# Sums of squares and scale exponents kept in spare PSUM columns, and only the last small VectorE step writing SBUF

## The chip, the cores and the metric

The kernel runs on one core of a Trainium2 chip. The metric is the device time of one execution in microseconds (us), lower is better. The engines are TensorE (PE in the profile, PEld for its weight loads), VectorE (DVE), ScalarE (ACT), GpSimd (POOL) and SyncE (SP, which issues most DMAs).

## The reference

Two stages, in float32. The first is a long convolution with gates: `u = x * v`; a filter `h_filt = (relu(pos_emb @ w1) @ w2) * exp(-0.01 * pos)`; `y = irfft(rfft(u) * rfft(h_filt))`, causal, over 12480 positions, for 2 batches and 128 channels; output `x * y`. The second is a feed-forward block on the 24960 tokens that come out: `h = x @ w_in` (128 to 2048), `g = max(h, 0) + alpha * min(h, 0)`, `g @ w_out`.

## The kernel before

Phase A computes the convolution by matmuls, as a Fourier transform of length 24960 = 195 x 128 in stages, with data split into two float16 parts (a high part and the remainder). The 128 channels come in two groups of 64. For each group **stage 1** forms `u`, scales it, splits it and multiplies with the table `t1`; **stage 2** (lines 674 to 808) multiplies with twiddles and with the filter's spectrum; **stage 3** (lines 813 to 874) goes back to tokens and stores to `g_d` in DRAM. Stage 1 of the second group runs together with stage 3 of the first. Phase B (from line 1024) finishes the transform per block of 390 tokens and runs the feed-forward block; it begins at about 640 us.

float16 has a narrow range, so each channel of `u` and of the filter gets a power-of-two scale. Stage 1 works in pairs of chunks (`u_pair`, 16 pairs per group, 32 in all; a pair is 8 channels): DMA loads x and v; `product` multiplies (L550, on DVE or POOL); `square` squares on ACT (L553); `norm` sums squares over the partitions on PE with a matrix of ones into a bank `mb` of PSUM (L561, 8 matmuls); `gather` sums 128 columns of that bank to 8 on DVE (L565, into the SBUF tile `n2`); `scale` runs the three small instructions of `scales` on DVE (L325 shifts the exponent out of `n2` into the SBUF tile `sc_e`, L326 clips and negates it in place, L327 adds a bias and writes `s_u`, in SBUF); `scaled` multiplies u with the scale (L576, on DVE or POOL); then `high` on ACT (L582), `low` on DVE or POOL (L585), the 48 matmuls of `transform` on PE (L619 to L621), and the reading of their bank by ACT (L631) and DVE (L634). The filter calls `scales` once, for 128 channels: L325 to L327 on 128 columns, then L401 scales `w2b`, for which PE waits in L419.

Each engine runs its instructions in the written order. That order comes from a list planner (`Plan`) which gives each operation a cost, its inputs (`r`), its outputs (`w`) and rooms: the pool "m" has two rooms, the two banks `mb`. A room is free again 200 ns after the planned end of the last operation that names it; before the change that is `gather` for a pair, since `scale` does not name the bank. In the second group's plan rooms are given in a fixed order.

In stage 3 (together with the second group's stage 1) DVE reads PSUM in L851 and PE works in L834 to L836.

Of the kernel before, what the change touches and what calls it, by code (L numbers as in the profile page):

```python
# [8 lines left out]
F32 = mybir.dt.float32  # L9
# [3 lines left out]
I32 = mybir.dt.int32  # L13
AF = mybir.ActivationFunctionType
ALU = mybir.AluOpType
AX = mybir.AxisListType
# [5 lines left out]
D = 128  # L22
# [14 lines left out]
CC = 4  # L37
# [212 lines left out]
def act_ns(n, psum=False):  # L250
    return n / 1.2 + (51 if psum else 93)


def dve_ns(n, rate=1):
    return n / 0.96 / rate + 67
# [6 lines left out]
def dma_ns(n):  # L262
    return n / 360
# [23 lines left out]
def body(ctx, tc, A, out, stop=None, dbg=None):  # L287
    nc = tc.nc
    sy, ac, ve, po, te = nc.sync, nc.scalar, nc.vector, nc.gpsimd, nc.tensor
# [12 lines left out]
    s_h = const.tile([128, D], F32, name="s_h")  # L302
# [14 lines left out]
    def units(u, n=1, p=128):  # L317
        assert u >= FIRST or u + n <= FIRST
        t, u = (ring, u - FIRST) if u >= FIRST else (first, u)
        return t[:p, u:u + n].rearrange("p u e -> p (u e)")  # L320

    def scales(pool, n2, s_out, n):

        e = pool.tile([128, n], I32, tag="sc_e", bufs=2, name="sc_e")
        ve.tensor_single_scalar(out=e, in_=n2.bitcast(I32), scalar=24, op=ALU.logical_shift_right)  # L325
        ve.tensor_scalar(out=e, in0=e, scalar1=10, scalar2=-(1 << 23), op0=ALU.max, op1=ALU.mult)  # L326
        ve.tensor_single_scalar(out=s_out.bitcast(I32), in_=e, scalar=196 << 23, op=ALU.add)  # L327

    def filter_(P, pool, z, mm, mb):
# [21 lines left out]
        w = ib * NT  # L351
# [41 lines left out]
        nh = P.buf("m")  # L393
# [3 lines left out]
            ve.tensor_scalar(out=nb, in0=ones, scalar1=n1, scalar2=float(FO), op0=ALU.mult, op1=ALU.mult)  # L397

        def scaled():
            scales(pool, mb[nh.i][:, :D], s_h, D)  # L400
            ve.tensor_tensor(out=w2b, in0=w2b, in1=s_h.unsqueeze(1).to_broadcast([128, 2, D]), op=ALU.mult)  # L401

        P.op("DVE", 400, gather, r=[("nq", q) for q in range(nq)], w=["nb"])
# [2 lines left out]
        for g in range(1, len(w2s)):  # L406
            P.op("ACT", act_ns(2 * D), lambda g=g: ac.activation(w2s[g], w2b, AF.Copy, scale=float(np.exp(-DECAY * WJ * g))),
                 r=[("w2s", 0)], w=[("w2s", g)])
# [95 lines left out]

    def phase_a():
        ps = ctx_a.enter_context(tc.tile_pool(name="psa", bufs=1, space=PSUM))
        wk = ctx_a.enter_context(tc.tile_pool(name="wk", bufs=2))
        mm = [ps.tile([128, 1024], F32, name=f"mm{j}") for j in range(3)]
        mb = [ps.tile([128, 512], F32, name=f"mb{j}") for j in range(2)]
        zp = ctx_a.enter_context(tc.tile_pool(name="zp", bufs=1))  # L510
# [11 lines left out]
        def stage1(P, g, shared, U):  # L522
            def u_pair(n):

                nps = P.buf("m")
                more = not shared and n >= NCH // 2 and n // 2 % 2
                kind = ("x2", "v2", "sq1", "uhl2") if more else ("x", "v", "sq1", "uhl")
                x, v, sq = [P.buf(kind[0]) for _ in range(2)], [P.buf(kind[1]) for _ in range(2)], P.buf(kind[2])
                b, c = divmod(n * CC, CG)
                c += g * CG  # L530
                s = s_u[:, b, c:c + 2 * CC]

                def xr(j):
                    return units(U[x[j].pool][x[j].i], p=NT)

                def vr(j):
                    return units(U[v[j].pool][v[j].i], p=NT)

                def sqr():
                    return units(U[sq.pool][sq.i], p=NT).bitcast(BF16).rearrange("p (c i) -> p c i", i=NI)  # L540

                n2 = []

                for j in range(2):
                    def load(j=j):
                        sy.dma_start(out=xr(j), in_=A["xv"][g, n + j, :, 0, :])
                        sy.dma_start(out=vr(j), in_=A["xv"][g, n + j, :, 1, :])

                    def product(e, j=j):
                        either[e].tensor_tensor(out=xr(j), in0=xr(j), in1=vr(j), op=ALU.mult)  # L550

                    def square(j=j):
                        ac.activation(sqr()[:, j * CC:j * CC + CC].rearrange("p c i -> p (c i)"), xr(j), AF.Square)  # L553

                    P.op("DMA", dma_ns(2 * NT * 2048), load, r=stored if more else [], w=[x[j], v[j]])
                    P.op({"DVE": dve_ns(512), "POOL": 1225}, 0, product, r=[v[j]], w=[x[j]])
                    P.op("ACT", act_ns(512), square, r=[x[j], sq], w=[("sq", n, j)])

                def norm():
                    for m in range(8):  # L560
                        te.matmul(mb[nps.i][:, :128], ones[:NT], sqr()[:, :, 16 * m:16 * m + 16], start=m == 0, stop=m == 7)  # L561

                def gather():
                    n2.append(wk.tile([128, 2 * CC], F32, tag="n2", name="n2"))
                    ve.tensor_reduce(out=n2[0], in_=mb[nps.i][:, :128].rearrange("p (c e) -> p c e", e=16), op=ALU.add, axis=AX.X)  # L565

                def scale():
                    scales(wk, n2[0], s, 2 * CC)

                P.op("PE", 450, norm, r=[sq, ("sq", n, 0), ("sq", n, 1)], w=[nps], rows=98)  # L570
                P.op("DVE", 220, gather, r=[nps], w=[("s", g, n)])
                P.op("DVE", 450, scale, w=[("s", g, n)])
                for j in range(2):
                    def scaled(e, j=j):
                        u = xr(j).rearrange("p (c i) -> p c i", c=CC)
                        either[e].tensor_tensor(out=u, in0=u, op=ALU.mult,  # L576
                                                in1=s[:NT, j * CC:(j + 1) * CC].unsqueeze(2).to_broadcast([NT, CC, NI]))

                    h = P.buf(kind[3])

                    def high(j=j, h=h):
                        ac.activation(halves(h)[:, 0], xr(j), AF.Copy)  # L582

                    def low(e, j=j, h=h):
                        either[e].tensor_tensor(out=halves(h)[:, 1], in0=xr(j), in1=halves(h)[:, 0], op=ALU.subtract)  # L585

                    P.op({"DVE": 600, "POOL": 1001}, 0, scaled, r=[("s", g, n)], w=[x[j]])
                    P.op("ACT", act_ns(512), high, r=[x[j]], w=[h])
                    P.op({"DVE": 600, "POOL": 1113}, 0, low, r=[x[j]], w=[h])
                    transform(n + j, [h], split(h))  # L590

            def halves(h):
                return units(U[h.pool][h.i], p=NT).bitcast(F16).rearrange("p (h e) -> p h e", h=2)

            def split(h):
                return lambda c, part: halves(h)[:, part, c * NI:(c + 1) * NI]
# [12 lines left out]
            def transform(n, keys, data):  # L609
                pb = P.buf("mm")  # L610
                col = n * CC
                zb, cs = z[:, col // ZC], slice(col % ZC, col % ZC + CC)
                late = [("rt", q) for q in range(16)] if not shared and CG <= col < NU else []

                def product():
                    p = mm[pb.i].rearrange("p (c j) -> p c j", c=CC)
                    for c in range(CC):
                        o = p[:, c, :2 * NF]
                        te.matmul(o, data(c, 0), t1[:, 0], start=True, stop=False)  # L619
                        te.matmul(o, data(c, 0), t1[:, 1], start=False, stop=False)  # L620
                        te.matmul(o, data(c, 1), t1[:, 0], start=False, stop=True)  # L621

                def pv():
                    return mm[pb.i].rearrange("p (c j) -> p c j", c=CC)[:, :, :2 * NF].rearrange("p c (a f) -> p a f c", a=2)

                P.op("PE", 12 * 84, product, r=keys, w=[pb] + late, rows=98)

                cuts = (0, 2 * FB, NF) if n == NCH - 1 or shared and n == NC // CC - 1 else (0, NF)
                for x, y in zip(cuts, cuts[1:]):
                    def high(x=x, y=y):  # L630
                        ac.activation(zb[:, 0, :, x:y, cs], pv()[:, :, x:y], AF.Copy)  # L631

                    def low(x=x, y=y):
                        ve.tensor_tensor(out=zb[:, 1, :, x:y, cs], in0=pv()[:, :, x:y], in1=zb[:, 0, :, x:y, cs], op=ALU.subtract)  # L634

                    P.op("ACT", act_ns(8 * (y - x), True), high, r=[pb], w=[("z", n, x)])
                    P.op("DVE", dve_ns(8 * (y - x)), low, r=[pb], w=[("z", n, x)])
# [258 lines left out]
        with tc.tile_pool(name="pre", bufs=2) as pre:  # L896
            P = Plan(mm=3, m=2, pt=5, x=8, v=3, sq1=2, uhl=4, x2=4, v2=2, uhl2=2)
# [16 lines left out]
        for g in range(1, NG):  # L914
            P = Plan(mm=3, m=2, x=7, v=3, sq1=2, uhl=3, sn=2, gst=2)
# [20 lines left out]
        P = Plan(mm=3, sn=3, gst=3)  # L936
# [295 lines left out]
```

## Time and profile before

| | us |
|---|---|
| median of 3 runs | 1831.11 (1825.75 to 1833.94) |
| profiled execution | 1827.88 |
| its span, first to last instruction | 1826.0 |
| PE busy | 1726.7 (95%) |
| VectorE busy | 1435.6 (79%) |
| ScalarE busy | 1298.5 (71%) |
| GpSimd busy | 1112.2 (61%) |

The shares are means over stages that differ: phase B (from 640 us) is 1186 us of PE at work, while in phase A VectorE is the engine with the least idle time over long stretches. Durations of an instruction include time in which it is held after it began, so that instructions of one form with the same data size can have different lengths.

### The profile page before, as it was taken

What the parts mean: (1) busy time and instruction counts of PE and PEld (TensorE: products, weight loads), DVE (VectorE), ACT (ScalarE), POOL (GpSimd) and SP (SyncE); (2) the same over time, 40 slices, a digit from 0 to 9 for tenths busy, and PEclk for the clock granted to TensorE, in tenths of its full rate; (3) what the DMA queues carried; (4) which work ended last, traced back from release to release, by engine and by line L of the source; (5) the groups of instructions that cost most, each with busy time, mean ns of one, the idle gap of its engine ahead of it and who ended that gap; (6) DMA issues with size and microseconds to landing.
All of it is one profiled execution on the core that took longest, in us unless ns stands there. A gap on an engine that the chain in (4) does not pass through costs nothing.

```text
span 1826.0 us, 34019 instructions
## 1 busy us (share of the span) xinstructions
PE 1726.7 (95%) x13398; PEld 1652.1 (90%) x13398; DVE 1435.6 (79%) x1660; ACT 1298.5 (71%) x1976; POOL 1112.2 (61%) x736
## 2 busy tenths in 40 slices
PE   7998888798888899999999999999999999999998
PEld 5997777787777799999999999999999999999998
DVE  5569999998997767777777777777777777777775
ACT  6457676676664477777777777777777777777776
POOL 4456988776893165556555655666555655565564
PEclk8779999899998999999999999999999999999999
DMA  6343345774434941010210120102101112012000
GB/s 192 99 124 109 137 149 157 212 237 150 162 127 120 256 131 54 18 54 28 62 53 19 54 64 26 54 18 72 54 19 53 32 58 54 19 54 64 26 9 19
DMA packets 98582, 155.05 MB, mean 85 GB/s; under 512 B 7088, under 2 KB 65746, under 8 KB 96468
## 3 DMA queue, kind: packets, MB, share of 16 engines
q1 hardware_dynamic: 97060, 152.05, 27.2%
q8 instruction: 105, 1.72, 0.4%
q10 hardware_dynamic: 1360, 0.81, 0.1%
q14 instruction: 57, 0.47, 0.1%
HBM read 106.97 MB, written 45.88 MB: 84 GB/s over the span
## 4 chain that ended last, share of the span: by engine, by line
PE 62%; DVE 19%; ACT 7%; DMA 6%; issue 6%; POOL 1%; ACTq 0%; POOLq 0%; SPq 0%; DVEq 0%
PE hp L1063 25%; PE o L1063 23%; DVE ring L733 5%; PE mm L419 4%; DVE ring L1127 3%; DVE ring L743 3%; ACT ring L1126 3%; DMA g_d<-ring 2%; DVE z L634 2%; DVE g_lo L1134 1%; ACT g_hi L1133 1%; PE yp L277 1%; PE yp L278 1%; PE yp L279 1%; PE mm L834 1%
## 5 line engine op out<-in xcount | busy, mean ns | idle before, releaser
L1134 POOL TENSOR_TENSOR g_lo<-ring,g_hi 128x780 fp32r<-128x780 f32 x256 | 506.6, 1979 | 494.6 <-ACT g_hi L1133 494.6
L1127 DVE SCALAR_TENSOR_TENSOR ring<-ring,keep,hp 128x780 f32<-128x780 f32 x512 | 523.8, 1023 | 284.6 <-ACT ring L1126 278.5
L1126 ACT ACTIVATE ring<-hp 128x780 f32<-128x780 f32 x512 | 420.4, 821 | 290.6 <-PE hp L1063 290.6
L1063 PE MATMUL hp<-ah,w 128*128 128x390 f32 x2048 | 543.1, 346 | 7.7 <-DVE ring L1127 2.9
L1063 PE MATMUL o<-g_hi,w 128*128 128x390 f32 x2048 | 534.6, 342 | 0.3 <-ACT ot L1148 0.3
L1133 ACT ACTIVATE g_hi<-ring 128x780 fp32r<-128x780 f32 x512 | 434.9, 849 | 0.4 <-DVE ring L1127 0.4
L1063 PEld LDWEIGHTS hp<-ah,w 128*128 128x128 f32 x2048 | 371.3, 190 | 24.0 <-DVE ring L1127 21.3
L1134 DVE TENSOR_TENSOR g_lo<-ring,g_hi 128x780 fp32r<-128x780 f32 x256 | 380.2, 1485 | 0.0
L1063 PEld LDWEIGHTS o<-g_hi,w 128*128 128x128 f32 x2048 | 375.1, 189 | 0.6 <-ACT ot L1148 0.6
L1063 PE MATMUL o<-g_lo,w 128*128 128x390 f32 x1024 | 266.4, 341 | 0.5 <-POOL g_lo L1134 0.5
L1063 PE MATMUL hp<-alo,w 128*128 128x390 f32 x1024 | 266.7, 342 | 0.0
L1063 PEld LDWEIGHTS o<-g_lo,w 128*128 128x128 f32 x1024 | 188.5, 189 | 0.8 <-POOL g_lo L1134 0.8
L1063 PEld LDWEIGHTS hp<-alo,w 128*128 128x128 f32 x1024 | 188.8, 189 | 0.1
L1049 POOL TENSOR_TENSOR gl<-gt,gh 98x1024 f16<-98x1024 f32 x62 | 134.2, 2164 | 3.8 <-ACT gh L1048 3.8
L733 DVE TENSOR_TENSOR ring<-mm,ring 128x512 f32<-128x512 f32 (+2 forms) x204 | 125.9, 656 | 8.4 <-ACT ring L721 8.1
L760 POOL TENSOR_TENSOR z<-ring,z 128x512 f16<-128x512 f32 x96 | 119.0, 1240 | 4.1 <-ACT z L756 4.1
L834 PE MATMUL mm<-t,z 128*128 128x128 f16 x512 | 104.5, 235 | 16.5 <-DVE z L634 7.5
L738 POOL TENSOR_TENSOR ring<-ring 128x256 f32<-128x256 f32 (+1 forms) x98 | 91.7, 936 | 46.4 <-DVE ring L733 41.6
L756 ACT ACTIVATE z<-ring 128x512 f16<-128x512 f32 (+2 forms) x102 | 62.5, 613 | 72.3 <-DVE ring L743 49.1
L836 PE MATMUL mm<-t,z 128*128 128x128 f16 x512 | 103.9, 234 | 0.1
L835 PE MATMUL mm<-t,z 128*128 128x128 f16 x512 | 104.0, 234 | 0.0
L619 PE MATMUL mm<-t,ring 98*128 98x196 f16 x320 | 84.3, 264 | 17.1 <-DVE z L634 7.9
(142 smaller groups left out, 3206.4 us busy)
## 6 DMA issues: line engine op xcount, KB each, us to landing
g_d<-ring SPq DMA_DIRECT2D x32, 784.0 KB
gt<-g_d SPq DMA_DIRECT2D x16, 1568.0 KB
ring<-in_tw SPq DMA_DIRECT2D x37, 512.0 KB
ring<-in_xv SPq DMA_DIRECT2D x72, 196.0 KB
xt<-in_xt SPq DMA_DIRECT2D x31, 390.0 KB
out_t<-ot SPq DMA_DIRECT2D x31, 390.0 KB
first<-in_xv SPq DMA_DIRECT2D x56, 196.0 KB
first<-in_tw SPq DMA_DIRECT2D x13, 512.0 KB
```

The costliest lines, as they stand in the source:

```text
L733: ve.tensor_tensor(out=t[:, :, m], in0=p[:, :, m], in1=hs[:, a:a + 1, m].to_broadcast([128, 2, (b1 - b0) * 2 * ZC]), op=ALU.mult)
L738: e.tensor_tensor(out=ta[:, 0, m], in0=ta[:, 0, m], in1=tb[:, 1, m], op=ALU.subtract)
L760: e.tensor_tensor(out=zl, in0=v, in1=zh, op=ALU.subtract)
L834: te.matmul(o, hi, t3[:, 0], start=True, stop=False)
L835: te.matmul(o, hi, t3[:, 1], start=False, stop=False)
L836: te.matmul(o, lo, t3[:, 0], start=False, stop=True)
L1049: po.tensor_tensor(out=dl, in0=src, in1=dh, op=ALU.subtract)
L1063: te.matmul(o[:, b, :TOK], w, d[:, b], start=start and n == 0, stop=stop and n == 2)
L1126: ac.activation(neg, h, AF.Relu, scale=-1.0)
L1127: ve.scalar_tensor_tensor(out=acts[n], in0=neg, scalar=keep[:, f:f + 1], in1=h, op0=ALU.mult, op1=ALU.add)
L1133: ac.activation(gh, a, AF.Copy)
L1134: (ve, po)[n % 2].tensor_tensor(out=gl, in0=a, in1=gh.bitcast(F32), op=ALU.subtract)
```

## The change

The tile `sc_e` (exponents) and the tile `n2` (sums) are no longer made in SBUF; the pool `wk` goes. `gather` writes its 8 sums into columns 256 to 263 of the pair's own bank `mb`, L325 writes the exponents into columns 264 to 271, L326 works there in place, and L327 reads them there and writes `s_u` or `s_h` in SBUF as before. For the filter the exponents go to columns 128 to 255 of its bank. The operation `scale` now names the bank, so that the planner keeps the room until `scale` has ended.

```diff
-    def scales(pool, n2, s_out, n):
-        e = pool.tile([128, n], I32, tag="sc_e", bufs=2, name="sc_e")
+    def scales(e, n2, s_out):
+        e = e.bitcast(I32)
         ve.tensor_single_scalar(out=e, in_=n2.bitcast(I32), scalar=24, op=ALU.logical_shift_right)
         ve.tensor_scalar(out=e, in0=e, scalar1=10, scalar2=-(1 << 23), op0=ALU.max, op1=ALU.mult)
         ve.tensor_single_scalar(out=s_out.bitcast(I32), in_=e, scalar=196 << 23, op=ALU.add)
...
-            scales(pool, mb[nh.i][:, :D], s_h, D)
+            scales(mb[nh.i][:, D:2 * D], mb[nh.i][:, :D], s_h)
...
-        wk = ctx_a.enter_context(tc.tile_pool(name="wk", bufs=2))
...
+                def spare(j):
+                    return mb[nps.i][:, 256 + 2 * CC * j:256 + 2 * CC * (j + 1)]
+
                 def gather():
-                    n2.append(wk.tile([128, 2 * CC], F32, tag="n2", name="n2"))
-                    ve.tensor_reduce(out=n2[0], in_=mb[nps.i][:, :128].rearrange("p (c e) -> p c e", e=16), op=ALU.add, axis=AX.X)
+                    ve.tensor_reduce(out=spare(0), in_=mb[nps.i][:, :128].rearrange("p (c e) -> p c e", e=16), op=ALU.add, axis=AX.X)
 
                 def scale():
-                    scales(wk, n2[0], s, 2 * CC)
+                    scales(spare(1), spare(0), s)
...
-                P.op("DVE", 450, scale, w=[("s", g, n)])
+                P.op("DVE", 450, scale, r=[nps], w=[("s", g, n)])
```

## Rows read from the trace of the kernel before

**Rows 1.** Windows by stage: start:end, length, each engine's busy us, clock, DMA, GB/s.
```profile
0.00:114.00 114.00, 102.56 (x612) 90.68 (x613) 62.41 (x98) 58.11 (x102) 47.33 (x44) 0.78 0.42 129
114.00:172.00 58.00, 47.43 (x515) 44.65 (x512) 56.13 (x81) 47.07 (x73) 46.23 (x39) 0.94 0.42 129
...
297.00:440.00 143.00, 120.71 (x1510) 115.01 (x1510) 125.41 (x199) 99.43 (x220) 99.43 (x85) 0.93 0.69 207
...
640.00:1826.00 1186.00, 1177.15 (x7604) 1151.20 (x7602) 898.12 (x824) 892.25 (x1143) 693.34 (x348) 1.00 0.15 45
```

**Rows 2.** Waits of PE from 114 to 172: us in total, times, longest.
```profile
PE mm L619 <- DVE z L634: 7.6, 9, 2.5
```

**Rows 3.** Waits of PE from 297 to 440.
```profile
PE mm L834 <- DVE z L634: 7.5, 5, 2.9
PE mm L619 <- DVE ring L851: 5.4, 4, 2.2
```

**Rows 4.** Instructions of the tile sc_e: durations ns min/median/max, first and last start.
```profile
L326 DVE TENSOR_SCALAR sc_e<-sc_e x33: 170/1029/1286, 20.0 to 422.4; 128x8 int32<-128x8 int32 x32, 128x128 int32<-128x128 int32 x1
L325 DVE TENSOR_SCALAR sc_e<-n x32: 154/214/1026, 19.8 to 422.2; 128x8 int32<-128x8 int32 x32
L327 DVE TENSOR_SCALAR s_u<-sc_e x32: 170/172/1111, 20.2 to 422.6; 128x8 int32<-128x8 int32 x32
```

**Rows 5.** Windows of the tile sc_e alone: VectorE busy us, then clock, DMA, GB/s.
```profile
0.00:114.00 114.00, 11.03 (x27) 0.78 0.42 129
114.00:172.00 58.00, 10.38 (x24) 0.94 0.42 129
297.00:440.00 143.00, 24.42 (x48) 0.93 0.69 207
```

**Rows 6.** Timeline, 29 to 33: start, us, engine, line, operation, shapes, [idle before].
```profile
29.07 3.71 POOL L550 TENSOR_TENSOR ring<-ring,first 98x512 f32<-98x512 f32 x3
...
30.07 0.29 DVE L325 TENSOR_SCALAR sc_e<-mb 128x128 int32<-128x128 int32 x1 [0.89 <-PE mb L404]
30.40 1.24 DVE L326 TENSOR_SCALAR sc_e<-sc_e 128x128 int32<-128x128 int32 x1
31.67 1.19 DVE L327 TENSOR_SCALAR s_h<-sc_e 128x128 int32<-128x128 int32 x1
```

**Rows 7.** Lines L634 and L565, which read PSUM and write SBUF.
```profile
L634 DVE TENSOR_TENSOR z<-mm,z x99: 223/964/980, 33.2 to 434.8; 128x784 f16<-128x784 f32 x93, 128x64 f16<-128x64 f32 x3, 128x720 f16<-128x720 f32 x3
L565 DVE TENSOR_REDUCE n<-mb x32: 273/278/284, 19.5 to 421.9; 128x8 f32<-128x128 f32 x32
```

**Rows 8.** Timeline of PE from 33.3.
```profile
33.38 2.88 PE L419 MATMUL mm<-w2b,z 128*98 128x128 f32 x12 [0.53 <-DVE w2b L401]
```

**Rows 9.** Chain of waits by line, windows 114:146, 311:346 and 373:424 in turn.
```profile
by line: DVE z L634 45.1%; DVE ring L550 10.0%; DVE sc_e L326 8.8%; POOL ring L576 6.4%; DVE sc_e L325 6.2%; issue 5.7%; ACT z L631 5.4%; DVE s_u L327 5.1%; DVE ring L576 4.3%; DVE n L565 1.9%; PE mm L619 1.6%; PE mm L621 1.1%; PE mm L620 1
by line: DMA g_d<-ring 31.7%; DVE ring L851 12.7%; DVE ring L576 8.8%; issue 8.0%; DVE z L634 7.9%; DVE sc_e L326 7.3%; DVE sc_e L325 5.9%; DVE ring L550 4.4%; DVE s_u L327 3.9%; PE mm L619 2.4%; ACT z L631 2.4%; PE mm L621 2.0%; PE mm L620
by line: DVE z L634 18.3%; DVE ring L851 12.7%; PE mm L834 8.2%; issue 8.2%; PE mm L835 7.2%; PE mm L836 7.1%; DVE sc_e L326 7.1%; PE mm L619 5.3%; PE mm L621 5.1%; PE mm L620 5.0%; DVE sc_e L325 2.8%; PE mb L561 2.7%; POOL ring L585 2.3%; 
```

**Rows 10.** Timeline, 154 to 163, of VectorE, GpSimd and PE.
```profile
154.81 0.52 DVE L325 TENSOR_SCALAR sc_e<-n 128x8 int32<-128x8 int32 x1
155.36 1.08 DVE L326 TENSOR_SCALAR sc_e<-sc_e 128x8 int32<-128x8 int32 x1
...
156.73 1.04 POOL L576 TENSOR_TENSOR ring<-ring,s_u 98x512 f32<-98x512 f32 x1 [0.31 <-DVE s_u L327]
...
161.74 1.01 PE L561 MATMUL mb<-ring,ones 98*128 98x128 bf16 x8 [2.54 <-ACT ring L553]
```

**Rows 11.** Lines L550 and L576 on VectorE, with two inputs from SBUF.
```profile
L550 DVE TENSOR_TENSOR ring<-ring,first x10: 672/693/1425, 27.4 to 404.9; 98x512 f32<-98x512 f32 x10
L576 DVE TENSOR_TENSOR ring<-ring,s_u x17: 675/875/1646, 21.9 to 424.4; 98x512 f32<-98x512 f32 x17
```

**Rows 12.** Timeline of VectorE and PE from 335.9.
```profile
335.91 1.35 PE L561 MATMUL mb<-ring,ones 98*128 98x128 bf16 x16
335.99 0.17 DVE L327 TENSOR_SCALAR s_u<-sc_e 128x8 int32<-128x8 int32 x1
```

More of the change, by code (lines that the diff above doesn't have):

```diff
@@ L540, in sqr @@
                     return units(U[sq.pool][sq.i], p=NT).bitcast(BF16).rearrange("p (c i) -> p c i", i=NI)
-                n2 = []
                 for j in range(2):
```

## The prediction

> **What bounds the kernel now.** I read the windows by stage first, since the page's mean shares mix stages. From 640 us PE is busy for 1177 of 1186 us, and nothing there is edited. The edited instructions stand in three stretches only: A, 0 to 114 us (the filter and the first pairs), B, 114 to 172 us (the rest of the first group's stage 1), C, 297 to 440 us (the second group's stage 1 beside stage 3). In B VectorE is busy for 56.1 of 58 us and PE for 47.4; in C VectorE for 125.4 of 143 and PE for 120.7 [rows 1]. The waits of PE say who leads: PE waits 7.6 us for L634 in B, and in C 7.5 us for L634 and 5.4 us for L851, both VectorE reading a bank that PE wants back [rows 2, 3]. So VectorE sets the pace of B and most of C. In A it doesn't: from 33.38 us on PE runs matmuls of L419 nearly without a gap, after an idle 0.53 us in which it waited for the filter's scales [rows 8].
>
> Then the tile view of the edited instructions. L326, on 8 columns, has a shortest duration of 170 ns and a median of 1029 [rows 4]. Such a difference at equal size is not work. The timeline shows its cause at 30 us: POOL runs three multiplications of L550 on end (29.07 to 32.78). In them, L325 reads 128 columns from PSUM, writes SBUF and takes 0.29 us; L326, on the same 128 columns from SBUF to SBUF, takes 1.24, and L327 1.19 [rows 6]. I read that as VectorE being held until a POOL instruction ends when it works SBUF to SBUF in this form, and not held when its input is PSUM. L565, PSUM to SBUF, agrees: 32 times between 273 and 284 ns, whatever POOL did [rows 7].
>
> **The change, part by part.** The number of instructions stays: 33 triples L325 to L327 and 32 L565.
>
> *Size of one small step.* L634 takes 964 ns for 784 columns and 223 for 64, so 741 / 720 = 1.03 ns a column [rows 7]. L325 from PSUM on 128 columns is 291 ns at most [rows 6], less 120 columns gives 167 ns for 8, beside 154 to 172 ns for an unheld step in SBUF [rows 4]. No row shows VectorE writing PSUM. From below 154 ns; from above 291 ns, the dearest unheld step here with a PSUM operand. I take 170, the nearest in size, so a step costs as before, without the hold. At the upper end 34 steps on the path (counted below) cost 34 x 0.12 = 4.1 us. L565 keeps its 278 ns.
>
> The Trainium skill, in "VectorE: DVE Perf Modes", section "The TRN2 errata", gives a PSUM source 62 cycles more of fixed cost than an SBUF source; as an estimate that is 65 ns a step, 2.2 us on the 34, and the time would be 1821.9. The 291 ns row speaks against it.
>
> *Whole gain on VectorE.* The steps are busy 11.03 + 10.38 + 24.42 = 45.8 us for 99 instructions [rows 5]; unheld 99 x 0.17 = 16.8, plus 0.3 for the filter's wide ones. 28.7 us of hold goes. How much of it counts goes by stretch.
>
> *A.* The filter's L326 and L327 fall from 2.43 to about 0.6 us, but PE idles only 0.53 us for them; the norms ahead of L419 fill the rest. Other triples there lie beside PE at work. Gain 0.5.
>
> *B.* The chain of waits from 114 to 146 gives L326, L325 and L327 8.8 + 6.2 + 5.1 = 20.1% of 32 us, 6.4 us [rows 9], in twelve pieces (four triples); unheld 12 x 0.17 = 2.0. Gain 4.4. After 146 the chain passes to POOL and PE, but POOL waits there for a scale: the triple at 154.81 is held 0.35 + 0.91 us, POOL's L576 starts right behind it, and through L550 and L553 PE's norm at 161.74, after 2.54 us of idle [rows 10]. Of 1.26 I count 0.9. B gives 5.3; all its hold would be 10.38 - 24 x 0.17 = 6.3.
>
> *C.* Chain from 311 to 346: 7.3 + 5.9 + 3.9 = 17.1% of 35 us = 5.98, twelve pieces, less 12 x 0.17 = 2.04, gain 3.9. From 373 to 424: 7.1 + 2.8 = 9.9% of 51 us = 5.05, ten pieces (L327's are unheld there), less 1.7, gain 3.3 [rows 9]. C gives 7.2; all its hold would be 24.42 - 48 x 0.17 = 16.3. Between 346 and 373 the chain runs over PE and I count nothing.
>
> *Holds that move.* Eight triples are followed at once by L550 or L576 on VectorE, which have two SBUF inputs and are held too: 672 and 675 ns unheld, up to 1425 and 1646 [rows 11]. Today the triple has often waited out the POOL instruction for them. Each may lose 0 to 0.97 us; I take the median excess of L576, 0.2, 1.6 in all.
>
> *The bank held longer.* `scale` now names the bank, so a norm must follow the scale of two pairs earlier. In the trace every norm already does, the closest being the second of the two that share the 16 matmuls at 335.91: it begins near 336.5, and the scale two pairs earlier ends at 336.16 [rows 12], itself a held one that ends earlier then. I cost it at nothing; if that cover fails it is the last rival. The freed pool and columns cost nothing: no DMA is added, and the instruction count of each engine is the same.
>
> Sum: 0.5 + 5.3 + 7.2 - 1.6 = 11.4 us. The profiled execution took 1827.9 (span 1826.0 and 1.9 around it), which gives 1816.5; it lies 3.2 below the median of the runs shown, so against that median 1819.7. What is late next is PE and ACT in C, and POOL's queue in B.
>
> **The rivals.**
>
> *The hold only moves to the last step.* L327 still writes SBUF. If a write to SBUF is what is held, L325 and L326 become short and L327 waits for the POOL instruction that L326 waits for today. The gain is then only the second and third holds of a triple, some 3 us on the path: 1828. For it: L327 has been held itself, up to 1111 ns [rows 4]. Against it: L325 from PSUM wrote SBUF unheld under POOL [rows 6]. This is also the case that the change doesn't do what it says.
>
> *Time freed on VectorE becomes idle time.* In C PE is busy 120.7 of 143 us, and ACT and the DMA of stores stand in the chain (31.7% of 311 to 346) [rows 1, 9]. If PE, ACT or POOL is just behind, half of C and a third of B go: 0.5 + 3.5 + 3.6 - 1.6 = 6.0, so 1825.
>
> *More than the chain shows.* PE's waits for VectorE in B and C are 20.5 us [rows 2, 3]; if all the hold of B and C turned into time, 0.5 + 6.3 + 16.3 - 1.6 = 21.5, 1810. For it: VectorE is the leader in both. Against it: the chain leaves VectorE for long pieces in C.
>
> *Slower: the planner writes another order.* A room of the pool m is free only when `scale` ends in the plan, some 0.5 to 2 us later than now. If the plan (which has its own costs, not those of the trace) finds the room shut, it puts a transform ahead of the norm, and that pair's scale, L576, L585 and matmuls all come later, with VectorE and POOL idle. The price is a PE wait as now seen behind L634, up to 2.9 us [rows 3], for each pair. From four pairs on the gain is gone; with eight in C 8 x 2.9 - 11.4 = +11.8, 1843. For it: one margin of 0.3 us [rows 12]. Against it: every other norm follows by 1.9 us or more.
>
> **How the numbers follow.** Chances: the forecast 0.45, hold moves 0.10, idle time 0.23, more than the chain 0.14, slower 0.08. 0.5% of 1831 is 9.2 us, about what a measurement can tell from no change, so faster means below 1822 and slower above 1840. The forecast, with its own 1814 to 1825 (upper step price, moved holds 0 to 0.97 each on half of the places), lies below 1822 in three quarters of its cases, 0.34; more than the chain adds 0.14 and idle time 0.08: faster 0.56. Slower has 0.07, its own case but for 0.01 where the loss only cancels the gain. The rest, 0.37, is the same. The range leaves out the far half of the large gain and the slower case: 1810 to 1831.
>
> **What would show it.** Right: no L326 above 0.25 us, L325 and L327 near 170 ns, 45.8 us of these steps near 17, B and C together about 12 us shorter, phase B as long as before. The hold moves: L327 with a median near 1 us. Idle time: steps short, but C no shorter and PE waiting for ACT or POOL. Another order: norms standing elsewhere among the matmuls, VectorE idle before L565. The forecast is wrong if the steps stay long, or if phase A ends within 5 us of where it ends now.

## The result, and the profile after

The changed kernel takes 1813.67 us (median of 4 runs, 1812.52 to 1817.52), the kernel before 1829.93 beside it. The ratio is 0.9915, 95% interval 0.9888 to 0.9942: 10.6 to 20.5 us less, 15.6 in the middle. The forecast was 11.4 us less. The profiled execution has a span of 1810.7 us, 15.3 below that of before. Every engine issues its instructions in the same order as before, so all differences come from how long they took and waited. (The edit moves line numbers: L550 is L547 after, L565 L564, L576 L575, L585 L584, L634 L633, L851 L850, L1063 L1062; L325 to L327 keep theirs.)

The small steps first: the view by tile `mb` of the kernel after, with durations in ns as min/median/max. It answers to [rows 4, 7].

```profile
L325 DVE TENSOR_SCALAR mb<-mb x33: 156/164/300, 21.1 to 409.9; 128x8 int32<-128x8 int32 x32, 128x128 int32<-128x128 int32 x1
L326 DVE TENSOR_SCALAR mb<-mb x33: 173/174/300, 21.3 to 410.1; 128x8 int32<-128x8 int32 x32, 128x128 int32<-128x128 int32 x1
L564 DVE TENSOR_REDUCE mb<-mb x32: 277/286/300, 20.8 to 409.5; 128x8 f32<-128x128 f32 x32
L327 DVE TENSOR_SCALAR s_u<-mb x32: 165/166/167, 21.5 to 410.3; 128x8 int32<-128x8 int32 x32
```

L326 had a median of 1029 ns, now 174; even its 128 columns take no more than 300 ns where they took 1.24 us [rows 6]. L327, which still writes SBUF, varies by 2 ns in 32 times. The steps' durations add up to 5.56 + 5.88 + 5.60 = 17.0 us, from 46.1 by the same sum. (The windows of [rows 5], which count overlaps once, have 45.8; they have 16.8 now.)

Next, where the time went. First matmul of each stage in the two traces (us), taken from the timeline of PE:

| | before | after | after minus before |
|---|---|---|---|
| last L419 of the filter | 109.5 | 110.2 | +0.7 |
| first group, stage 2 | 171.9 | 168.8 | -3.1 |
| stage 3 of it, beside stage 1 of the second | 301.0 | 297.9 | -3.1 |
| second group, stage 2 | 434.0 | 420.9 | -13.1 |
| last of stage 3 | 622.8 | 607.3 | -15.5 |
| first of phase B | 629.0 | 611.8 | -17.2 |
| end of the span | 1826.0 | 1810.7 | -15.3 |

B gave 3.8 us, C 10.0. The 2.4 us between 434 and 623 and the 1.7 behind it lie in unedited code, and phase B is 1.9 longer. In four kernels run below (the three variants of the small steps and the one with added shifts), which differ from this one only in the stretches A to C, the length from the second group's stage 2 to the last matmul of stage 3 was 187.3 to 189.5, beside 188.8 before and 186.4 here. I take that part as spread between executions; nothing shows it to be the change's.

Windows of B and C cut at these edges, the kernel before and then after (columns as in [rows 1]: PE, PEld, VectorE, ScalarE, GpSimd busy us).

```profile
113.60:171.90 58.30, 47.73 (x521) 44.95 (x519) 56.14 (x82) 47.32 (x73) 46.62 (x39) 0.94 0.43 130
297.10:435.00 137.90, 115.71 (x1450) 110.17 (x1450) 123.72 (x197) 96.53 (x215) 99.33 (x85) 0.93 0.68 204
```

```profile
114.50:168.80 54.30, 48.17 (x522) 45.20 (x520) 49.49 (x81) 46.74 (x73) 47.48 (x39) 0.93 0.46 144
294.00:421.90 127.90, 115.14 (x1451) 109.40 (x1450) 109.81 (x197) 96.28 (x216) 99.93 (x85) 0.93 0.73 219
```

VectorE's busy time fell by 6.7 us in B and 13.9 in C, that of PE, ScalarE and GpSimd hardly moved, and VectorE's idle time rose from 2.2 to 4.8 and from 14.2 to 18.1 us. So 4.0 of 6.7 and 10.0 of 13.9 us turned into time. PE's waits for VectorE in C were 14.2 us (7.5, 5.4, 0.7 and 0.6, from 301 to 435). Now they are 3.1, and a wait for a DMA, 0.7 us before, is longer than any of them (the kernel after, 297 to 435):

```profile
PE mm L618 <- DMA ring<-h_d: 3.9, 3, 1.8
PE mm L618 <- DVE ring L850: 1.5, 4, 0.6
PE mm L705 <- DVE z L633: 0.6, 1, 0.6
PE mm L618 <- DVE z L633: 0.6, 2, 0.4
PE mm L833 <- DVE ring L850: 0.4, 2, 0.2
```

(One more wait for VectorE, 2.8 us before and 2.5 after, stands ahead of the first small step of C and stays.)

C has 16 triples, the 17th to the 32nd of stage 1, so its parts can be compared between the same instructions (us, the number of a triple in brackets):

| part of C | before | after | gain | forecast |
|---|---|---|---|---|
| to the start of (17) | 10.0 | 9.5 | 0.6 | 0 |
| start of (17) to end of (22), 311 to 343 | 32.1 | 28.7 | 3.5 | 3.9 |
| end of (22) to start of (25), 343 to 373 | 29.5 | 25.5 | 4.0 | 0 |
| start of (25) to end of (32), 373 to 423 | 50.1 | 48.9 | 1.2 | 3.3 |
| from there to stage 2 | 11.2 | 10.4 | 0.8 | 0 |

The third and fourth parts went otherwise than forecast. Windows of these two, before and then after:

```profile
343.10:372.60 29.50, 24.74 (x297) 24.42 (x295) 24.20 (x37) 20.60 (x46) 19.96 (x17) 0.83 0.67 203
372.65:422.78 50.13, 42.86 (x575) 41.30 (x573) 47.97 (x80) 38.68 (x85) 42.76 (x37) 1.00 0.76 228
```

```profile
336.00:361.50 25.50, 25.09 (x326) 24.56 (x325) 22.42 (x37) 20.38 (x46) 20.24 (x17) 0.91 0.84 248
361.54:410.45 48.91, 44.23 (x567) 42.59 (x565) 40.83 (x80) 37.93 (x83) 43.06 (x37) 0.95 0.77 236
```

In the third part PE was idle for 4.8 of 29.5 us before and for 0.4 of 25.5 after. Its waits there were 2.9 us for L634 and 1.9 for L851, and the granted clock of the stretch was 0.83 before, 0.91 after: the idle time between held VectorE instructions had been followed by PE at 1.2 GHz. The chain of before showed this stretch as PE's, so I had counted nothing. In the fourth part VectorE is busy 7.1 us less, and 5.9 of that is idle time now. The chain of waits there (kernel after, 361.5 to 410, by line) says what took over:

```profile
by line: DMA first<-in_xv 32.7%; DMA ring<-h_d 17.3%; POOL ring L584 13.2%; issue 7.0%; PE mm L618 5.8%; POOL ring L547 5.6%; PE mm L620 5.0%; PE mm L619 4.8%; SPq L544 3.9%; SPq L543 3.3%; PE mb L558 3.0%; PE mm L834 1.6%; PE mm L833 1.6%;
```

No VectorE line stands in it. It is a loop: GpSimd's L584 reads the last of a buffer, SyncE can load the next x and v into it, GpSimd's L547 waits for them. A second thing happened at the end of this part: PE, which now waits for the loads of `h_d`, was idle for 1.84 us, and the granted clock, 1.00 in this part up to 405.3 us, was 0.50 (1.2 GHz) from there to its end, with PE on the chain. Timeline of PE:

```profile
402.35 0.61 PE L558 MATMUL mb<-ring,ones 98*128 98x128 bf16 x8
404.79 0.26 PE L618 MATMUL mm<-t,ring 98*128 98x196 f16 x1 [1.84 <-DMA ring<-h_d]
...
408.48 1.01 PE L558 MATMUL mb<-ring,ones 98*128 98x128 bf16 x8
```

Window from 405.3 to the end of the part:

```profile
405.30:410.45 5.15, 5.15 (x37) 4.47 (x35) 2.69 (x7) 3.20 (x5) 3.44 (x4) 0.50 0.42 122
```

In the kernel before, the whole part ran at 1.00. The eight matmuls of L558 took 0.61 us at the upper level and 1.01 at the lower; by that, as an estimate, some 2 of the 5.15 us can be the clock, about as much as this part fell short by. The runs do not separate it from the loop.

Holds that moved, in the list of groups of the whole span, before and then after (count | busy us, mean ns):

```profile
L576 DVE TENSOR_TENSOR ring<-ring,s_u 98x512 f32<-98x512 f32 x17 | 17.8, 1055 | 0.4
L550 DVE TENSOR_TENSOR ring<-ring,first 98x512 f32<-98x512 f32 x10 | 8.6, 856 | 0.0
```

```profile
L575 DVE TENSOR_TENSOR ring<-ring,s_u 98x512 f32<-98x512 f32 x17 | 19.2, 1137 | 0.4
L547 DVE TENSOR_TENSOR ring<-ring,first 98x512 f32<-98x512 f32 x10 | 10.8, 1083 | 1.6 <-DMA first<-in_xv 1.6
```

These two-input instructions got 3.6 us longer, 1.9 of it in the nine that stand right behind a triple (the prediction counted eight): some of the wait that a triple used to sit out falls on the next instruction with two SBUF inputs.

### The profile page after: what moved, and what is told of

Same layout as the page of the kernel before. It is cut to its first block, busy times and chain, and to the rows that moved or that the text cites. A ratio compares the mean times of both kernels' runs of the same rounds, so it can differ in the third digit from the quotient of the medians.

```text
span 1810.7 us, 34020 instructions
## 1 busy us (share of the span) xinstructions
PE 1727.5 (95%) x13398; PEld 1653.5 (91%) x13398; DVE 1411.7 (78%) x1660; ACT 1298.0 (72%) x1976; POOL 1114.2 (62%) x736
## 4 chain that ended last, share of the span: by engine, by line
PE 62%; DVE 16%; ACT 7%; issue 6%; DMA 6%; POOL 3%; SPq 1%; POOLq 0%; ACTq 0%; DVEq 0%
PE hp L1062 25%; PE o L1062 23%; DVE ring L732 5%; PE mm L419 4%; DVE ring L742 3%; DVE ring L1126 3%; ACT ring L1125 3%; POOL ring L584 2%; DVE g_lo L1133 1%; ACT g_hi L1132 1%; PE yp L277 1%; PE yp L278 1%; PE yp L279 1%; DMA first<-in_xv 1%; PE mm L833 1%
## 5 line engine op out<-in xcount | busy, mean ns | idle before, releaser
L1062 PE MATMUL hp<-ah,w 128*128 128x390 f32 x2048 | 543.9, 347 | 8.8 <-DMA w<-w_d 4.7
L1062 PE MATMUL o<-g_hi,w 128*128 128x390 f32 x2048 | 534.5, 342 | 0.3 <-ACT ot L1147 0.3
L1062 PEld LDWEIGHTS hp<-ah,w 128*128 128x128 f32 x2048 | 371.6, 190 | 25.3 <-DVE ring L1126 22.8
L1062 PEld LDWEIGHTS o<-g_hi,w 128*128 128x128 f32 x2048 | 375.1, 189 | 0.6 <-ACT ot L1147 0.6
L1062 PE MATMUL hp<-alo,w 128*128 128x390 f32 x1024 | 266.9, 342 | 0.0
L1062 PE MATMUL o<-g_lo,w 128*128 128x390 f32 x1024 | 266.4, 341 | 0.5 <-POOL g_lo L1133 0.5
L1062 PEld LDWEIGHTS hp<-alo,w 128*128 128x128 f32 x1024 | 189.2, 190 | 0.1
L1062 PEld LDWEIGHTS o<-g_lo,w 128*128 128x128 f32 x1024 | 188.5, 189 | 0.8 <-POOL g_lo L1133 0.8
L737 POOL TENSOR_TENSOR ring<-ring 128x256 f32<-128x256 f32 (+1 forms) x98 | 91.8, 937 | 46.5 <-DVE ring L732 42.1
L633 DVE TENSOR_TENSOR z<-mm,z 128x784 f16<-128x784 f32 (+1 forms) x99 | 91.6, 941 | 14.2 <-ACT z L630 13.4
```

Of the source, the lines that this page charges most:

```text
L737: e.tensor_tensor(out=ta[:, 0, m], in0=ta[:, 0, m], in1=tb[:, 1, m], op=ALU.subtract)
L1062: te.matmul(o[:, b, :TOK], w, d[:, b], start=start and n == 0, stop=stop and n == 2)
```

## The experiments

**Who holds, and what is held.** Theory: GpSimd's instructions hold a VectorE step that has its input and its output in SBUF. First, GpSimd taken away: the kernel before, with stage 1's either-engine operations planned on VectorE alone.

```diff
-  P.op({"DVE": dve_ns(512), "POOL": 1225}, 0, product, ...)
+  P.op({"DVE": dve_ns(512), "POOL": 1e7}, 0, product, ...)
...
-  P.op({"DVE": 600, "POOL": 1001}, 0, scaled, ...)
+  P.op({"DVE": 600, "POOL": 1e7}, 0, scaled, ...)
...
-  P.op({"DVE": 600, "POOL": 1113}, 0, low, ...)
+  P.op({"DVE": 600, "POOL": 1e7}, 0, low, ...)
```

> The kernel before, with stage 1's multiplications, scalings and subtractions planned on VectorE alone (GpSimd's cost set out of reach), so that GpSimd has none of them; the small steps stay SBUF to SBUF. Much slower (160 operations of 0.67 us or more go over to VectorE: 1880 to 1980). Theory: the hold is by GpSimd's instructions, so L326 falls to a median of 170 ns and L325, L327 too, though nothing moved to PSUM; at most a few near the ends of stage 2 stay long. Rival: the hold is the step's own wait for the result just before it in SBUF, and L326 stays near 1 us.

Measured: 1898.48 us, one run. The small steps and L576, all in SBUF as before (view by line):

```profile
L325 DVE TENSOR_SCALAR sc_e<-n x32: 157/161/171, 20.4 to 487.7; 128x8 int32<-128x8 int32 x32
L326 DVE TENSOR_SCALAR sc_e<-sc_e x33: 170/171/227, 20.6 to 487.9; 128x8 int32<-128x8 int32 x32, 128x128 int32<-128x128 int32 x1
L327 DVE TENSOR_SCALAR s_u<-sc_e x32: 170/171/173, 20.8 to 488.1; 128x8 int32<-128x8 int32 x32
L576 DVE TENSOR_TENSOR ring<-ring,s_u x64: 662/682/693, 22.4 to 489.6; 98x512 f32<-98x512 f32 x64
```

No step is held any more, without a byte moved to PSUM. The long durations are GpSimd's doing, and a wait for the step just before is ruled out. (The planner also wrote another order for this kernel, but no step of it is long.) It also gives the price of the unheld step in SBUF, 161 to 171 ns, beside 164 to 174 in PSUM after the change. On the filter's 128 columns it is otherwise: 227 ns in SBUF here, up to 300 in PSUM after the change, so a wide step does pay for PSUM.

The traces show the hold step by step as well. Of the 96 steps on 8 columns in the kernel before, 38 took over 200 ns, and each of them ended 24 to 33 ns after the end of a GpSimd instruction; of the other 58 a single one lay inside a GpSimd instruction. After the change 58 of the 96 lay wholly inside a GpSimd instruction, and none took more than 175 ns.

Then the change taken apart. The sums stay in PSUM, the exponents go back to SBUF:

```diff
...
-                    scales(spare(1), spare(0), s)
+                    scales(wk.tile([128, 2 * CC], F32, tag="sc_e", bufs=2, name="sc_e"), spare(0), s)
...
-            scales(mb[nh.i][:, D:2 * D], mb[nh.i][:, :D], s_h)
+            scales(pool.tile([128, D], F32, tag="sc_e", bufs=2, name="sc_e"), mb[nh.i][:, :D], s_h)
```

> Only half of the change: the sums stay in PSUM, the exponents go back to SBUF, so L325 goes PSUM to SBUF and L326, L327 go SBUF to SBUF. Theory: a small step is held by GpSimd only when both its input and its output are in SBUF. Then L325 is short (near 165 ns in all 32), L326 is held again with a median near 1 us, L327 sometimes; L326 now also waits out what L325 waited for before, so the steps of the triples are busy 38 to 45 us, and the time is 1822 to 1829. Rival 1, any SBUF operand is enough for a hold: L325 is held too, up to 1 us, and the time is that of the kernel before, 1830. Rival 2, what counts is where the sums lie: time as after the change, 1814.

Measured: 1823.9 us, ratio 0.9963 (0.9949 to 0.9977). L325 and L326:

```profile
L325 DVE TENSOR_SCALAR sc_e<-mb x33: 147/155/292, 21.1 to 417.5; 128x8 int32<-128x8 int32 x32, 128x128 int32<-128x128 int32 x1
L326 DVE TENSOR_SCALAR sc_e<-sc_e x33: 171/352/1324, 21.3 to 417.7; 128x8 int32<-128x8 int32 x32, 128x128 int32<-128x128 int32 x1
```

PSUM to SBUF is not held (16 of the 32 lay inside a GpSimd instruction), SBUF to SBUF is, as expected; all steps add up to 40.6 us. The median of L326 was expected near 1 us and is 0.35.

The other half: the sums go back to SBUF, the exponents stay in PSUM.

```diff
...
-                    ve.tensor_reduce(out=spare(0), in_=mb...
+                    n2.append(wk.tile([128, 2 * CC], F32, tag="n2", name="n2"))
+                    ve.tensor_reduce(out=n2[0], in_=mb...
...
-                    scales(spare(1), spare(0), s)
+                    scales(spare(1), n2[0], s)
```

> The other half: the exponents stay in PSUM, the sums go back to SBUF, so L325 goes SBUF to PSUM, L326 PSUM to PSUM, L327 PSUM to SBUF. Theory (held only with both ends in SBUF): all three short, 155 to 185 ns, triples busy near 17 us, time 1811 to 1817, so that moving the sums brought nothing. Rival, reading SBUF is enough for a hold: L325 goes up to 1 us with a median above 0.5 us, the steps are busy 28 to 35 us, time 1819 to 1825.

Measured: 1813.83 us, ratio 0.991 (0.9893 to 0.9926), the same as the whole change. L325:

```profile
L325 DVE TENSOR_SCALAR mb<-n x32: 151/158/170, 22.5 to 410.9; 128x8 int32<-128x8 int32 x32
```

SBUF to PSUM is not held either (20 of the 32 lay inside a GpSimd instruction). One end in PSUM is enough, and moving the sums brought nothing. The third variant leaves a single held step, the last:

```diff
...
-        ve.tensor_scalar(out=e, in0=e, scalar1=10, scalar2=-(1 << 23), op0=ALU.max, op1=ALU.mult)
-        ve.tensor_single_scalar(out=s_out.bitcast(I32), in_=e, scalar=196 << 23, op=ALU.add)
+        ve.tensor_scalar(out=e2, in0=e, scalar1=10, scalar2=-(1 << 23), op0=ALU.max, op1=ALU.mult)
+        ve.tensor_single_scalar(out=s_out.bitcast(I32), in_=e2, scalar=196 << 23, op=ALU.add)
...
```

(`e2` is a tile in SBUF.)

> As after the change, but L326 writes its result to SBUF, so that only L327 goes SBUF to SBUF. Theory: L325 and L326 short, L327 held with a median of 0.5 to 1.1 us; one hold in a triple where before there were up to three; the steps are busy 30 to 38 us and the time is 1819 to 1826, one hold costing most of what three cost since the first one waits out the GpSimd instruction. Rival, holds add up step by step and each is worth a third: time near 1819 with steps near 26 us. Rival 2, L327 is not held since it follows unheld steps closely: time 1814.

Measured: 1816.51 us, ratio 0.9924 (0.9907 to 0.994). L327:

```profile
L327 DVE TENSOR_SCALAR s_u<-sc_e x32: 170/188/1172, 20.0 to 412.5; 128x8 int32<-128x8 int32 x32
```

I had expected one hold to cost most of what three cost. It doesn't, nor is each worth a third: all steps add up to 23.5 us, so one step that can be held per triple costs 6.5 us over 17.0, two (the first variant) 23.6, three (before) 29.1. In time these kernels are some 1.6, 8.8 and 15.6 us behind the changed one, going by the ratios; the 1.6 is within the spread. Half of the 32 single steps found GpSimd free; the other 16 waited out the rest of one instruction and took 586 ns on average. A step held right behind another held one took longer, 964 to 1215 ns in the kernel before, which fits GpSimd starting its next instruction between them, so that a whole one is waited out. But in the sum the second step need not pay more: in the kernel before L325 lost 7.0 us to holds, L326 15.9, L327 6.2, in the first variant L326 12.1 and L327 11.7. Why the first step of a row loses 6.5 us in one variant and 12.1 in the other stays open.

**Is it VectorE's time alone?** Time of about the same size is put back, in PSUM:

```diff
                     scales(spare(1), spare(0), s)
+                    for j in range(4):
+                        ve.tensor_single_scalar(out=spare(2 + j).bitcast(I32), in_=spare(0).bitcast(I32), scalar=24, op=ALU.logical_shift_right)
```

> As after the change, with four more shifts from PSUM to PSUM behind each of the 32 triples of stage 1 (results unused): 128 x 0.2 us = 25.6 us of VectorE time, about the hold that went (28.7 us), put back without the SBUF side. The order on all engines is otherwise the same. Theory A: the hold was worth only VectorE's own time: the gain goes again, 1825 to 1831. Rival B: the hold also kept GpSimd or its loads back, and VectorE's time as such is worth little now: 1814 to 1820, with GpSimd's loop of loads setting the pace in the second group's stage 1.

Measured: 1824.54 us (12 runs), ratio 0.9974 (0.9963 to 0.9985), just below the range of theory A. The added shifts:

```profile
L569 DVE TENSOR_SCALAR mb<-mb x128: 173/174/175, 22.1 to 421.9; 128x8 int32<-128x8 int32 x128
```

From one start to the next they take 0.21 us, 26.6 in all. Of the 15.6 us, 10.7 are gone again. In the profile, which is of the slowest of the 12 runs (1829.85), B is 5.4 us longer than after the change for 6.7 us added there, C 6.2 for 13.3. So most of the gain is VectorE's time as such. About 5 us are left; the added time is 2.4 us short of the hold that went (29.0), which at the same rate is some 1 us, and the other 4 stay open (where in the order the time falls, or GpSimd).

**Is GpSimd next in line, so that moving its work to VectorE pays?** Three runs lower the handicap with which the planner keeps the either-engine operations off VectorE:

```diff
-            P.urge, P.patience, P.bias = 3, 50, 1377
+            P.urge, P.patience, P.bias = 3, 50, 1100
...
-            P.urge, P.patience, P.bias = 3, 50, 1377
+            P.urge, P.patience, P.bias = 3, 50, 400
...
-            P.urge, P.patience, P.bias = .5, 100, 1112
+            P.urge, P.patience, P.bias = .5, 100, 500
```

> After the change, with the planner's handicap on VectorE in the second group's plan lowered from 1377 to 1100 ns: 4 of GpSimd's operations go to VectorE and the order shifts. Theory: VectorE has idle time now in the second group's stage 1 and GpSimd with its loop of loads is next in line, so a little less on GpSimd gives 1806 to 1813. Rival: a new order loses as much as it gains: 1812 to 1822.

> The same with a handicap of 400 ns: 14 operations (13 of them the subtraction that frees a load buffer) go from GpSimd to VectorE, some 14 us less on GpSimd and 10 to 14 us more on VectorE, which had 18 us idle there. Theory (GpSimd and its loads are next in line): 1803 to 1812. Rival (VectorE is as near the limit as GpSimd): 1814 to 1822.

> After the change, with the first group's handicap lowered from 1112 to 500 ns: 13 operations go from GpSimd to VectorE there. Theory: in the first group's stage 1 the chain after the change runs over GpSimd from 137 to 162 us with VectorE idle for some 5 us, so 1809 to 1814. Rival: VectorE fills up first and PE waits for its reads of PSUM again: 1815 to 1822.

Measured: 1816.56 (ratio 0.9924, 0.9898 to 0.995), 1823.76 (0.9971, 0.995 to 0.9992) and 1825.23 (0.9955, 0.9931 to 0.998). The theory fell: none gains, two lose, and those two end a little above their rivals' ranges. In the second (handicap 400) the waits of GpSimd grew. From 290 to 430, after the change and then in this run:

```profile
POOL ring L547 <- DMA first<-in_xv: 12.8, 12, 3.1
...
POOL ring L575 <- DVE s_u L327: 4.0, 2, 2.1
```

```profile
POOL ring L547 <- DMA first<-in_xv: 23.9, 11, 4.1
...
POOL ring L575 <- DVE s_u L327: 13.6, 7, 2.8
```

My reading is that the loop is GpSimd, load buffer and load, and that a subtraction which VectorE does later frees its buffer later too. It is not shown: the order of all engines changes with each handicap, and these runs do not separate the two. In the third (first group) stage 2 starts at 178.4 us, 168.8 after the change, and PE's waits for L633 ahead of it are 6.5 us, 2.5 after the change, though VectorE is busy for only 54.7 of 64.4 us there.

**Does it hold elsewhere?** Stage 2 has VectorE busy for 120.7 of 122 us (172 to 294, after), and there the sum for the imaginary part has two SBUF inputs. One of them is put in a PSUM bank that stage 2 leaves free; its product is split in two for that. The control splits the product and keeps both halves in SBUF.

```diff
-                for t, a in ((ta, 0), (tb, 1)):
+                for t, a in ((ta, 0), (tb, 1))[:1 if f0 < NF - 4 else 2]:
                     ve.tensor_tensor(out=t[:, :, m], in0=p[:, :, m], in1=hs[:, a:a + 1, m]...
+                if f0 < NF - 4:
+                    for o, a in ((tb[:, 1, m], 1), (mb[1][:, m], 0)):    # control: tb[:, 0, m]
+                        ve.tensor_tensor(out=o, in0=p[:, a, m], in1=hs[:, 1, m], op=ALU.mult)
...
-    in1=tb[:, 0, m], op=ALU.add)
+    in1=mb[1][:, m] if f0 < NF - 4 else tb[:, 0, m], op=ALU.add)         # control: tb[:, 0, m]
```

> After the change, and the same idea where VectorE is busiest: in stage 2 (VectorE busy 123.6 of 125 us in the first group) the addition of the imaginary part has two SBUF inputs, 128x256 each, and a mean of 916 ns in 49 instructions. For all but the last two pairs of frequencies of a group one input is written to a bank of PSUM that stage 2 does not use, so that the addition has one SBUF input; for that one product of 512 columns is split in two of 256. Theory: the addition falls to about 430 ns (the 223 ns of 64 columns and 192 columns more at 1.03 ns), the two halves of the product are 430 each in place of 675, so 0.30 us less VectorE per pair, 47 pairs in each of two groups: 28 us if VectorE stays the bound; GpSimd with 109 of 125 us busy is next, so 14 to 28 us below the time after the change: 1786 to 1800. Rival: the hold of GpSimd moves elsewhere (its own instructions start and end at the same times, GpSimd or PE set the pace): 1808 to 1815.

> The control to the run before: the product is split in two in the same way, but both halves stay in SBUF, so that the addition keeps its two SBUF inputs. Theory: the addition stays held (a mean of 0.75 us or more) and VectorE gets 94 x 0.18 = 17 us more to do, 1820 to 1835. Rival: splitting alone shortens the holds, since VectorE arrives later behind a GpSimd instruction: at or below 1814.

Measured: 1801.2 us, ratio 0.9857 (0.9835 to 0.988), the fastest version here, some 12 us below the change alone (12.5 by the medians, 10.6 by the ratios to the kernel before, which was run beside each); the control 1836.29 (one run), just above its range. Groups of VectorE and GpSimd from 172 to 294, after the change:

```profile
L742 DVE TENSOR_TENSOR ring<-ring 128x256 f32<-128x256 f32 (+1 forms) x49 | 44.9, 916 | 0.7
L493 DVE SCALAR_TENSOR_TENSOR ring<-ring 128x512 int32<-128x512 int32 x4 | 2.7, 675 | 0.0
L737 POOL TENSOR_TENSOR ring<-ring 128x256 f32<-128x256 f32 (+1 forms) x48 | 45.3, 944 | 19.6 <-DVE ring L732 17.6 <-PE mm L708 2.0
```

With the sum's input in PSUM (L746 is the sum, L736 the halves, L741 is GpSimd's L737):

```profile
L736 DVE TENSOR_TENSOR mb<-mm,ring 128x256 f32<-128x256 f32 x47 | 19.7, 419 | 0.0
L746 DVE TENSOR_TENSOR ring<-ring,mb 128x256 f32<-128x256 f32 x47 | 19.4, 413 | 0.6
L736 DVE TENSOR_TENSOR ring<-mm,ring 128x256 f32<-128x256 f32 x46 | 18.9, 411 | 0.0
L493 DVE SCALAR_TENSOR_TENSOR ring<-ring 128x512 int32<-128x512 int32 x4 | 4.4, 1101 | 0.0
L741 POOL TENSOR_TENSOR ring<-ring 128x256 f32<-128x256 f32 (+1 forms) x49 | 37.7, 770 | 17.1 <-DVE ring L736 14.9 <-DVE ring L732 1.2 <-PE mm L708 1.0
```

The control:

```profile
L746 DVE TENSOR_TENSOR ring<-ring 128x256 f32<-128x256 f32 x43 | 42.3, 983 | 0.6
L493 DVE SCALAR_TENSOR_TENSOR ring<-ring 128x512 int32<-128x512 int32 x4 | 4.4, 1102 | 0.0
L741 POOL TENSOR_TENSOR ring<-ring 128x256 f32<-128x256 f32 x43 | 33.8, 786 | 27.6 <-DVE ring L736 27.6
```

The sum falls from 916 to 413 ns, and the halves cost what was expected. This kernel and the control have the same order on every engine and differ in one operand, so the 35 us between them are the operand's, as far as one run of the control tells. GpSimd's instruction beside the sum gets shorter too, 944 to 770, but not because of the operand: it is 786 in the control, where the sum is held. That VectorE holds GpSimd in turn shows elsewhere: with the sum's input in PSUM, the four L741 of the first group that began while VectorE ran L501, which has two SBUF inputs, took 1171 to 1192 ns, and 41 of the other 43 took 722 to 749. The gain is just below the range (12 where 14 to 28 was expected), since the weights' conversions (lines 488 to 501), all from SBUF to SBUF, got longer: 43.0 us of VectorE in both groups after the change, 61.4 here. They come to 61.8 in the control, so this is a cost of the split and not of the operand. VectorE's account is 44.6 us saved on the sums, 14.9 spent on the halves and 18.4 on the conversions, 11.3 saved in all, near what was measured. First-group stage 2 took 121.6 us, from 129.1; with the split alone 143.2.

## Why the prediction was right

- **The cause of the long steps**, read from one moment at 30 us [rows 6] and one line [rows 7], was right, and is shown now: without GpSimd no step is held, with one end in PSUM none is, and each held step ends with a GpSimd instruction. The Trainium skill says it in "SBUF — State Buffer", section "Who interferes with whom": an instruction of VectorE with at most one SBUF input, outside the two-port modes, does not contend with GpSimd, while one in a two-port mode, or one with two SBUF inputs beside a GpSimd instruction that reads SBUF, does. The traces agree: 165 to 167 ns for L327 from PSUM, up to 1172 from SBUF; 413 ns for the sum with one SBUF input, 983 with two. In which mode a step ran, no trace here shows.
- **The size of a step**: 170 ns taken, 164 to 174 measured. The rule of the Trainium skill's "VectorE: DVE Perf Modes", section "The TRN2 errata", that I had weighed, 62 cycles more for a PSUM source, does not show on 8 columns: 161 to 171 ns in SBUF unheld, 164 to 174 in PSUM.
- **VectorE's time**: 28.7 us of hold forecast, 29.0 measured (45.8 less 16.8 in the windows of [rows 5]).
- **A**: 0.5 us forecast. PE's wait of 0.53 us ahead of L419 is gone, but L419 starts at 33.4 in both traces, and between 31.2 and 34.6 in the kernels above, so what that was worth can't be told here.
- **B**: 5.3 forecast. Between the starts of the 9th triple's L325 and the end of the 14th the stretch is 31.9 us after and 37.1 before: 5.3. Then 1.3 is given back before stage 2 starts, in the part that I had named as next, GpSimd's queue and PE behind it: 3.8 to stage 2.
- **C**, the term that was mis-sized: 7.2 forecast, 10.0 measured. The chain was right from 311 to 343 (3.9, measured 3.5), too high from 373 on (3.3, measured 1.2), where the loop of GpSimd and loads was just behind and PE's clock fell at the end, and blind between 343 and 373 (0, measured 4.0), where it ran over PE: by its waits of 2.9 and 1.9 us PE was late because of VectorE, and it then ran at the lower clock. That is read from the two traces; no run tests it by itself. A chain names who was busy last, not what had made that engine late.
- **Moved holds**: 1.6 us on the path forecast; right behind a triple 1.9 us measured, in all two-input instructions of these lines 3.6. How much of it lies on the path is not shown. With this term the forecast of B and C was 10.9 us, and 13.8 were measured.
- **The rivals.** The hold did not move to L327. The planner kept its order, so the slower case had no object. "Idle time" holds for the end of B and one part of C, "more than the chain" for another part of C. That the total came out so near is in part luck: B fell short by 1.5 us and the fourth part of C by 2.1, and the third part brought 4.0 that were not forecast.

The forecast of 1819.7 lies 6 us above the 1813.7 measured; its gain of 11.4 us lies inside the interval of 10.6 to 20.5. 2.2 us of the difference between the two profiles are in unedited code and not explained by the change.

## What to carry to other kernels

Where an instruction's shortest duration is a sixth of its median at equal size, look at what GpSimd does in that moment: a VectorE instruction with SBUF at both ends, or with two SBUF inputs, may be waiting for it, and one operand in a spare PSUM column ends that (one input, where there are two). Check whether the long ones end when a GpSimd instruction ends. Look for it first where VectorE is busiest, and don't price held steps one by one: a hold right behind another lasts a whole GpSimd instruction. What is done to make room for the operand has its own price, as the split in stage 2 shows. Price the gain stretch by stretch, and in stretches where the chain runs over PE ask whether PE is late because of the engine that you speed up.

## What was not expected of the hardware

One step per triple that can be held cost 6.5 us in all, two 23.6, three 29.1. A held step ended 24 to 33 ns after the GpSimd instruction it waited for, in each of 38 cases. VectorE writes 256 float32 columns to PSUM in 419 ns and to SBUF in 411, from the same kind of inputs.
